# One recurrent-attention kernel: three groups of TensorE products run as two 64-column tiles of the array instead of one full-width product

## The chip, the core and the metric

The kernel runs on one NeuronCore of one Trainium2 chip. A core has five engines that run side by side and wait for each other through semaphores: TensorE (PE, matrix products; the profile lists its weight loads apart as PEld), VectorE (DVE), ScalarE (ACT), GpSimd (POOL) and SyncE (SP, which here only issues DMAs). The metric is device time in microseconds (us) for one execution; lower is better. All data are 32-bit floats, and TensorE does every such product in two passes: in the trace each product of the program stands as two weight loads (LDWEIGHTS) and two MATMULs, a transpose as one of each.

## What is computed

A gated linear recurrence, and behind it a layer norm with a two-layer MLP and a residual. The sizes are batch 4, 8 heads, 768 tokens, 48 values per head, model width 384 and hidden width 1536.

```python
for t in range(S):
    state = alpha[:, :, t, :, None] * state + np.einsum('bhd,bhe->bhde', k[:, :, t], v[:, :, t])
    y[:, :, t] = np.einsum('bhd,bhde->bhe', q[:, :, t], state)
x = y.transpose(0, 2, 1, 3).reshape(B, S, H * D)
xn = (x - mean) / np.sqrt(var + 1e-06) * g_ln
out = x + np.maximum(xn @ w_ch1, 0.0) @ w_ch2
```

## The kernel before

The 768 tokens are cut into 6 chunks `c` of 128 (`NCB`), and a chunk's attention is done for each of the 4 batches `b` in six steps. Two heads always share a 128-wide slot: head 0 of a pair lies in positions 0 to 47, head 1 in 64 to 111, and the rest are zeros. There are 4 pairs `p` (`NP`).

- `decays` (lines 167 to 187): logarithm of alpha (ACT), a product with a triangle of ones for running sums (`lps`, line 173), two exponentials, q and k times those (`qks`), and two small DMAs that turn the last row of the decay into the columns `gate`. It also issues the loads of the next chunk.
- `turn` (line 194): eight transposes into `tps`, copied to `qkT` by ACT and DVE.
- `scores` (line 209): q times k per head into `aps`. Its two heads use rows 0 to 47 and 64 to 111 of the array, so they are two row tiles side by side. DVE keeps the lower triangle (`at`, line 212).
- `attend`: into `yps`, per pair, the state's part (line 221: stationary `qkT`, 128 columns; moving `sts`, 96 columns; chunks 1 to 5 only) and per head the scores' part (line 225: stationary `at`, 128 columns; moving v, 48 columns). Then x (ACT, line 228), the norm's statistics (DVE and ACT, lines 231 to 235) and the normed `xn` (DVE, line 237).
- `turn_x` (line 247): three transposes into `xps`, and DVE writes them to `xT` (line 248), which holds all four batches.
- `update` (line 257, chunks 0 to 4): per pair `sps`, k times v (stationary 128 columns, moving 96). It also makes products across the two heads of a pair, which aren't wanted. POOL makes `gm` (line 262), the gate times a mask `own` that is zero for those; DVE adds `sps` to the state `sts` (line 267; in chunk 0 it copies, line 265), and POOL multiplies the state by `gm` (line 268).

The MLP of a chunk has 12 steps `hidden` (line 278: 3 products of 512 columns, into `hps`, then a ReLU by ACT or DVE in turn) and 12 steps `project` (line 291: 4 products of 384 columns each, three steps to a batch, into `ops`, then DVE adds x, line 295). `hidden` needs `xT` of all four batches.

The order is written out by `run(main, side)`: behind every step of `main` it issues as many steps of `side` as keep the two lists level. `attention_steps` lists the steps in waves (`stages[w - b]` for batch `b` in wave `w`), so with 4 batches and 6 stages there are 24 steps. While the MLP of chunk `c` is `main` (24 steps), the attention of chunk `c+1` is `side` (24 steps). At the start the attention of chunk 0 is `main` and the rounding of the MLP's weights, which arrive as 64-bit floats, is `side` (seven DVE operations for a piece, lines 127 to 136). In the MLP of chunk 0, 6 of the 24 side steps go with the 12 `hidden` steps and 18 with the 12 `project` steps.

```python
            due = (i + 1) * len(side) // len(main)
            for go in side[done:due]:
                go()
```

The framework that builds the program from this text may move an instruction ahead of others on its engine where those have to wait. PSUM buffers with the tag `s` (`yps`, `sps`, `xps`) are two.

Of the kernel before, what the change touches and what calls it, by code (L numbers as in the profile page):

```python
# [9 lines left out]
FP32 = mybir.dt.float32  # L10
# [11 lines left out]
def kernel(  # L22
# [23 lines left out]

    nc = tc.nc

    B, S, H, D = q.shape
    DM = H * D
    DF = w_ch1.shape[1]
    P = 128
    NCB = S // P
    NP = H // 2
    NF = DM // P
    NJ = DF // P
    assert S % P == 0 and H % 2 == 0 and D <= 64 and DM % P == 0 and DF % P == 0
# [11 lines left out]

    r = np.arange(P)
    upto = (r[None, :] >= r[:, None]).astype(np.float32)
    half = np.stack([r < 64, r >= 64], 1).astype(np.float32)
    const_np = np.concatenate([upto, np.eye(P, dtype=np.float32), half], 1)

    raws = {}

# [4 lines left out]
            nc.sync.dma_start(t, src[b, c * P:(c + 1) * P])  # L83
            raws[n, c, b] = t

    consts = cpool.tile([P, 2 * P + 2], FP32, name="consts")
    nc.scalar.dma_start(consts, nc.inline_tensor(const_np, name="consts").ap())
    tri, ident, own = consts[:, :P], consts[:, P:2 * P], consts[:, 2 * P:]
# [73 lines left out]

    gate_of, qkT_of, at_of, x_of, xn_of, xT_of, hT_of = ({} for _ in range(7))
# [3 lines left out]
    def decays(c, b):  # L167
# [12 lines left out]
        if c + 1 < NCB:  # L180
            row = dram.tile([1, NP, P], FP32, name="row", tag="row")
            gate = work.tile([P, NP], FP32, name="gate", tag="gate", bufs=B)
# [4 lines left out]
            load(c + 1, b)  # L187

    def turn(c, b):
        qkT = work.tile([P, 2, NP, P], FP32, name="qkT", tag="qkT", bufs=3)  # L190
        for i in range(2):
            tps = ps.tile([P, NP, P], FP32, name="tps", tag="a", bufs=3)
            for p in range(NP):
                nc.tensor.transpose(tps[:, p], qks[b][:, i, p].rearrange("p a b -> p (a b)"),  # L194
                                    ident)
            if i == 0:
                nc.scalar.copy(out=qkT[:, i], in_=tps)
            else:
                nc.vector.tensor_copy(out=qkT[:, i], in_=tps)  # L199
        qkT_of[c, b] = qkT  # L200
# [13 lines left out]
        at_of[c, b] = at  # L214

    def attend(c, b):
        qkT, at, vt = qkT_of.pop((c, b)), at_of.pop((c, b)), raws["v", c, b]
        yps = ps.tile([P, NP, 2, D], FP32, name="yps", tag="s")
        for p in range(NP):
            if c > 0:  # L220
                nc.tensor.matmul(yps[:, p].rearrange("p a b -> p (a b)"), qkT[:, 0, p],  # L221
                                 sts[b][:, p].rearrange("p a b -> p (a b)"),
                                 start=True, stop=False)
            for i in range(2):
                nc.tensor.matmul(yps[:, p, i], at[:, i, p], vt[:, 2 * p + i],  # L225
                                 start=(c == 0), stop=(c == 0 or i == 1))
        x = work.tile([P, DM], FP32, name="x", tag="x", bufs=2 * B)
        nc.scalar.copy(out=x, in_=yps.rearrange("p a b d -> p (a b d)"))  # L228
        stats = work.tile([P, 6], FP32, name="stats", tag="stats")
        mv = work.tile([P, 2], FP32, name="mv", tag="mv")  # L230
        nc.vector.bn_stats(stats, x)  # L231
# [3 lines left out]
        nc.scalar.activation(out=rstd, in_=rstd, func=AFT.Exp, scale=-0.5)  # L235
        xn = work.tile([P, DM], FP32, name="xn", tag="xn", bufs=2)
        nc.vector.tensor_scalar(out=xn, in0=x, scalar1=mv[:, 0:1], scalar2=rstd,
                                op0=AOP.subtract, op1=AOP.mult)
        x_of[c, b], xn_of[c, b] = x, xn

    def turn_x(c, b):
        if b == 0:
            xT_of[c] = work.tile([P, NF, B, P], FP32, name="xT", tag="xT")
        xn = xn_of.pop((c, b))
        xps = ps.tile([P, NF, P], FP32, name="xps", tag="s")
        for f in range(NF):
            nc.tensor.transpose(xps[:, f], xn[:, f * P:(f + 1) * P], ident)  # L247
        nc.vector.tensor_mul(xT_of[c][:, :, b], xps,
                             g_col.unsqueeze(2).broadcast_to([P, NF, P]))

    def update(c, b):
        vt = raws.pop(("v", c, b))
        if c == NCB - 1:
            return
        sps = ps.tile([P, NP, 2, D], FP32, name="sps", tag="s")
        for p in range(NP):
            nc.tensor.matmul(sps[:, p].rearrange("p a b -> p (a b)"),  # L257
                             qks[b][:, 1, p].rearrange("p a b -> p (a b)"),
                             vt[:, 2 * p:2 * p + 2].rearrange("p a b -> p (a b)"),
                             start=True, stop=True)  # L260
        gm = work.tile([P, NP, 2], FP32, name="gm", tag="gm")
        nc.gpsimd.tensor_mul(gm, gate_of.pop((c, b)).unsqueeze(2).broadcast_to([P, NP, 2]),
                             own.unsqueeze(1).broadcast_to([P, NP, 2]))
        if c == 0:
            nc.vector.tensor_copy(out=sts[b], in_=sps)  # L265
        else:
            nc.vector.tensor_add(sts[b], sps, sts[b])  # L267
        nc.gpsimd.tensor_mul(sts[b], sts[b],  # L268
                             gm.unsqueeze(3).broadcast_to([P, NP, 2, D]))

# [87 lines left out]
```

## Time and profile before

| what | value |
|---|---|
| time, median of 3 runs | 578.32 us (572.75 to 579.47) |
| the profiled execution | 577.86 us |
| its span, first to last instruction | 576.1 us |
| mean granted TensorE clock | 0.964 |
| PE busy | 547.2 us, 95%, 2408 MATMULs |
| PEld busy | 342.1 us, 59%, 2408 loads |
| DVE busy | 222.7 us, 39% |
| ACT busy | 90.2 us, 16% |
| POOL busy | 55.2 us, 10% |

The busy shares are means over stages that differ. "Chain" below is the chain of work that ended last: the profile follows it back from the last instruction, at each step to what released it or to the instruction before it on its engine. A MATMUL's own duration in the trace (about 0.28 us for a small one) holds its way through the array; several are in flight at once, so the time that one costs in a row of them is read from the start of one to the start of the next, or from the chain.

### The profile page before, as it was taken

The page shows a single profiled execution, that of the slowest core. Times are in us where ns is not written, and L with a number is a line of the kernel's source. Part 1 is how long each engine was busy: PE and PEld are TensorE (multiplying, and loading weights), DVE is VectorE, ACT ScalarE, POOL GpSimd, SP SyncE. Part 2 cuts the span into 40 slices and gives each one's busy share as a digit, 9 for nine tenths or more (in the row PEclk, how much of TensorE's full clock was granted, in tenths as well). Part 3 has the DMA queues.
Part 4 walks back from the last instruction along what each step waited for, and adds up shares of the span by engine and source line. Part 5 has one row for each costly group of instructions (what it writes and reads, how often), then busy time and mean ns, then how long its engine had stood idle before and what let it go on. Part 6 is the DMA issues. An engine that isn't in the chain of part 4 may idle for free.

```text
span 576.1 us, 5992 instructions
## 1 busy us (share of the span) xinstructions
PE 547.2 (95%) x2408; PEld 342.1 (59%) x2408; DVE 222.7 (39%) x365; ACT 90.2 (16%) x205; POOL 55.2 (10%) x70
## 2 busy tenths in 40 slices
PE   4876897999999999999999999999999999999997
PEld 2675443667746567755567656566755566644453
DVE  3997997533343232233332223423223332211100
ACT  3311121111122200032210032210013210001000
POOL 2111131000110000020000120000111000000000
PEclk9865799999999999999999999999999999999999
DMA  8874433110231100032100122000000000000000
GB/s 284 285 213 133 151 109 96 43 56 27 65 87 42 41 28 29 27 91 62 41 21 22 41 70 69 28 1 28 14 15 0 1 0 22 21 14 0 0 29 27
DMA packets 32484, 33.64 MB, mean 58 GB/s; under 512 B 13108, under 2 KB 28596, under 8 KB 32456
## 3 DMA queue, kind: packets, MB, share of 16 engines
q1 hardware_dynamic: 31912, 33.12, 18.8%
q8 instruction: 19, 0.31, 0.2%
q10 hardware_dynamic: 544, 0.13, 0.1%
q14 instruction: 9, 0.07, 0.0%
HBM read 28.49 MB, written 4.76 MB: 58 GB/s over the span
## 4 chain that ended last, share of the span: by engine, by line
PE 84%; DVE 9%; DMA 5%; SPq 1%; issue 0%; ACT 0%; ACTq 0%
PE ops L291 33%; PE hps L278 28%; PE yps L225 7%; PE aps L209 4%; PE yps L221 3%; PE tps L194 3%; PE sps L257 3%; PE lps L173 2%; DMA row<-eq 2%; DVE ws L135 1%; DVE w L129 1%; DMA rv<-in_v_dram 1%; PE xps L247 1%; DMA ws<-in_moe_w_ch_dram 1%; DVE w L136 1%; DVE ws L134 1%
## 5 line engine op out<-in xcount | busy, mean ns | idle before, releaser
L278 PE MATMUL hps<-xT,w 128*128 128x512 f32 x432 | 198.3, 602 | 3.6 <-DVE hT L283 3.6
L291 PE MATMUL ops<-w,hT 128*128 128x384 f32 x576 | 198.7, 491 | 2.0 <-DVE ob L295 2.0
L291 PEld LDWEIGHTS ops<-w,hT 128*128 128x128 f32 x576 | 104.7, 190 | 66.0 <-DVE ob L295 4.1
L278 PEld LDWEIGHTS hps<-xT,w 128*128 128x128 f32 x432 | 80.4, 193 | 89.3 <-issue 78.3
L225 PE MATMUL yps<-rv,at 128*128 128x48 f32 x384 | 58.5, 283 | 2.4 <-DVE st L265 1.9
L225 PEld LDWEIGHTS yps<-rv,at 128*128 128x128 f32 x384 | 54.8, 209 | 3.8 <-DVE st L265 2.3
L283 DVE TENSOR_SCALAR hT<-hps 128x512 f32<-128x512 f32 x36 | 24.8, 690 | 57.7 <-PE hps L278 57.7
L178 POOL TENSOR_TENSOR qk<-rk,ek 128x384 f32<-128x384 f32 x24 | 30.2, 1259 | 165.3 <-ACT ek L176 160.4
L281 ACT ACTIVATE hT<-hps 128x512 f32<-128x512 f32 x36 | 21.5, 597 | 148.7 <-PE hps L278 148.7
L231 DVE BATCH_NORM_STATS2 stats<-x 128x6 f32<-128x384 f32 x24 | 13.4, 560 | 73.1 <-ACT x L228 73.1
L179 DVE TENSOR_TENSOR qk<-rq,eq 128x384 f32<-128x384 f32 x24 | 24.1, 1002 | 41.3 <-ACT eq L177 41.3
L228 ACT COPY x<-yps 128x384 f32<-128x384 f32 x24 | 11.5, 479 | 172.8 <-PE yps L225 172.8
L212 DVE COPY_PREDICATED at<-consts,aps 128x512 f32<-128x512 int32 x48 | 32.5, 717 | 13.5 <-PE aps L209 13.5
L268 POOL TENSOR_TENSOR st<-st,gm 128x384 f32<-128x384 f32 x20 | 18.1, 904 | 202.6 <-DVE st L267 181.3
L295 DVE TENSOR_TENSOR ob<-ops,x 128x384 f32<-128x384 f32 x24 | 13.4, 558 | 61.8 <-PE ops L291 61.8
L209 PEld LDWEIGHTS aps<-qkT 48*128 48x128 f32 x384 | 25.9, 202 | 16.9 <-issue 10.3
L209 PE MATMUL aps<-qkT 48*128 48x128 f32 x384 | 31.0, 302 | 3.0 <-DVE qkT L199 3.0
L194 PEld LDWEIGHTS tps<-consts,qk 128*128 128x128 f32 x192 | 23.5, 148 | 16.4 <-issue 8.2
L221 PE MATMUL yps<-st,qkT 128*128 128x96 f32 x160 | 32.7, 286 | 0.0
L194 PE MATMUL tps<-consts,qk 128*128 128x128 f32 x192 | 27.6, 286 | 4.9 <-DVE qk L179 4.2
L221 PEld LDWEIGHTS yps<-st,qkT 128*128 128x128 f32 x160 | 25.6, 192 | 6.2 <-issue 3.8
L199 DVE COPY qkT<-tps 128x512 f32<-128x512 f32 x24 | 16.6, 690 | 31.5 <-PE tps L194 31.5
(34 smaller groups left out, 281.8 us busy)
## 6 DMA issues: line engine op xcount, KB each, us to landing
ws<-in_moe_w_ch_dram SPq DMA_DIRECT2D x12, 768.0 KB
ra<-in_alpha_dram SPq DMA_DIRECT2D x24, 192.0 KB
rk<-in_k_dram SPq DMA_DIRECT2D x24, 192.0 KB
rq<-in_q_dram SPq DMA_DIRECT2D x24, 192.0 KB
rv<-in_v_dram SPq DMA_DIRECT2D x24, 192.0 KB
out_dram<-ob SPq DMA_DIRECT2D x24, 192.0 KB
row<-eq SPq DMA_DIRECT2D x20, 2.0 KB
gate<-row SPq DMA_DIRECT2D x20, 2.0 KB
```

Of the source, the lines that this page charges most:

```text
L178: nc.gpsimd.tensor_mul(qk[:, 1, :, :D], raws.pop(("k", c, b)), ek)
L179: nc.vector.tensor_mul(qk[:, 0, :, :D], raws.pop(("q", c, b)), eq)
L194: nc.tensor.transpose(tps[:, p], qks[b][:, i, p].rearrange("p a b -> p (a b)"), ident)
L209: nc.tensor.matmul(aps[i][:, p], qkT[rows, 1, p], qkT[rows, 0, p], start=True, stop=True)
L212: nc.vector.copy_predicated(out=at[:, i], data=aps[i], mask=mask.unsqueeze(1).broadcast_to([P, NP, P]))
L221: nc.tensor.matmul(yps[:, p].rearrange("p a b -> p (a b)"), qkT[:, 0, p], sts[b][:, p].rearrange("p a b -> p (a b)"), start=True, stop=False)
L225: nc.tensor.matmul(yps[:, p, i], at[:, i, p], vt[:, 2 * p + i], start=(c == 0), stop=(c == 0 or i == 1))
L268: nc.gpsimd.tensor_mul(sts[b], sts[b], gm.unsqueeze(3).broadcast_to([P, NP, 2, D]))
L278: nc.tensor.matmul(hps, w1[:, f, j * P:(j + 1) * P], xT_of[c][:, f], start=(f == 0), stop=(f == NF - 1))
L281: nc.scalar.activation(out=hT_of[c][:, j], in_=hps, func=AFT.Relu)
L283: nc.vector.tensor_scalar_max(hT_of[c][:, j], in0=hps, scalar1=0.0)
L291: nc.tensor.matmul(ops_of[b], hT_of[c][:, j, b], w2[:, j], start=(j == 0), stop=(j == NJ - 1))
```

## The change

The 128 columns of a stationary operand are cut in two halves of 64, each of which goes to its own half of the array's columns and writes its own 64 partitions of PSUM.

- `attend`: each product of lines 221 and 225 becomes two, one for tokens 0 to 63 and one for tokens 64 to 127 (`sides`), with the same moving operand. Of the 128 rows of the state's part 112 are used (`R`).
- The update moves from its own step into `attend`, right behind the products of y. Instead of one product per pair there is one per head (moving 48 columns instead of 96): head 0 on columns 0 to 63, head 1 on 64 to 111. The products across heads are no longer made, so the mask `own` and `gm` go. DVE adds in two pieces of 64 and 48 partitions, in chunk 0 as well, for which POOL clears `sts` at the start. POOL multiplies the state by the gate directly.
- `turn`: `qkT` and `tps` have 112 partitions instead of 128.
- `attention_steps`: five stages, 20 steps instead of 24, so `run` spreads them differently.

```diff
+    R = 64 + D
...
-    consts = cpool.tile([P, 2 * P + 2], FP32, name="consts")
+    consts = cpool.tile([P, 2 * P], FP32, name="consts")
...
+        nc.gpsimd.memset(sts[b], 0.0)
...
-        qkT = work.tile([P, 2, NP, P], FP32, name="qkT", tag="qkT", bufs=3)
+        qkT = work.tile([R, 2, NP, P], FP32, name="qkT", tag="qkT", bufs=3)
         for i in range(2):
-            tps = ps.tile([P, NP, P], FP32, name="tps", tag="a", bufs=3)
+            tps = ps.tile([R, NP, P], FP32, name="tps", tag="a", bufs=3)
             for p in range(NP):
-                nc.tensor.transpose(tps[:, p], qks[b][:, i, p].rearrange("p a b -> p (a b)"),
-                                    ident)
+                nc.tensor.transpose(
+                    tps[:, p], qks[b][:, i, p].rearrange("p a b -> p (a b)")[:, :R], ident)
...
+        sides = [slice(64 * s, 64 * s + 64) for s in range(2)]
         for p in range(NP):
             if c > 0:
-                nc.tensor.matmul(yps[:, p].rearrange("p a b -> p (a b)"), qkT[:, 0, p],
-                                 sts[b][:, p].rearrange("p a b -> p (a b)"),
-                                 start=True, stop=False)
+                for s in sides:
+                    nc.tensor.matmul(yps[s, p].rearrange("p a b -> p (a b)"), qkT[:, 0, p, s],
+                                     sts[b][:R, p].rearrange("p a b -> p (a b)"),
+                                     start=True, stop=False)
             for i in range(2):
-                nc.tensor.matmul(yps[:, p, i], at[:, i, p], vt[:, 2 * p + i],
-                                 start=(c == 0), stop=(c == 0 or i == 1))
+                for s in sides:
+                    nc.tensor.matmul(yps[s, p, i], at[:, i, p, s], vt[:, 2 * p + i],
+                                     start=(c == 0), stop=(c == 0 or i == 1))
+        if c + 1 < NCB:
+            sps = ps.tile([R, NP, D], FP32, name="sps", tag="s")
+            heads = list(enumerate((slice(0, 64), slice(64, R))))
+            for p in range(NP):
+                for i, s in heads:
+                    nc.tensor.matmul(sps[s, p], qks[b][:, 1, p, i, :s.stop - s.start],
+                                     vt[:, 2 * p + i], start=True, stop=True)
+            for i, s in heads:
+                nc.vector.tensor_add(sts[b][s, :, i], sps[s], sts[b][s, :, i])
+            st = sts[b].rearrange("p a b d -> p a (b d)")
+            nc.gpsimd.tensor_mul(
+                st, st, gate_of.pop((c, b)).unsqueeze(2).broadcast_to([P, NP, 2 * D]))
         x = work.tile([P, DM], FP32, name="x", tag="x", bufs=2 * B)
         nc.scalar.copy(out=x, in_=yps.rearrange("p a b d -> p (a b d)"))
...
-    def update(c, b):
...
-        sps = ps.tile([P, NP, 2, D], FP32, name="sps", tag="s")
-        for p in range(NP):
-            nc.tensor.matmul(sps[:, p].rearrange("p a b -> p (a b)"),
-                             qks[b][:, 1, p].rearrange("p a b -> p (a b)"),
-                             vt[:, 2 * p:2 * p + 2].rearrange("p a b -> p (a b)"),
-                             start=True, stop=True)
-        gm = work.tile([P, NP, 2], FP32, name="gm", tag="gm")
-        nc.gpsimd.tensor_mul(gm, gate_of.pop((c, b)).unsqueeze(2).broadcast_to([P, NP, 2]),
-                             own.unsqueeze(1).broadcast_to([P, NP, 2]))
-        if c == 0:
-            nc.vector.tensor_copy(out=sts[b], in_=sps)
-        else:
-            nc.vector.tensor_add(sts[b], sps, sts[b])
-        nc.gpsimd.tensor_mul(sts[b], sts[b],
-                             gm.unsqueeze(3).broadcast_to([P, NP, 2, D]))
...
-        stages = [decays, turn, scores, attend, turn_x, update]
+        stages = [decays, turn, scores, attend, turn_x]
```

More of the change, by code (lines that the diff above doesn't have):

```diff
@@ L73 @@
     upto = (r[None, :] >= r[:, None]).astype(np.float32)
-    half = np.stack([r < 64, r >= 64], 1).astype(np.float32)
-    const_np = np.concatenate([upto, np.eye(P, dtype=np.float32), half], 1)
+    const_np = np.concatenate([upto, np.eye(P, dtype=np.float32)], 1)
     raws = {}
@@ L84, in load @@
             raws[n, c, b] = t
-    consts = cpool.tile([P, 2 * P + 2], FP32, name="consts")
+    consts = cpool.tile([P, 2 * P], FP32, name="consts")
     nc.scalar.dma_start(consts, nc.inline_tensor(const_np, name="consts").ap())
-    tri, ident, own = consts[:, :P], consts[:, P:2 * P], consts[:, 2 * P:]
+    tri, ident = consts[:, :P], consts[:, P:]
     mask = tri.bitcast(INT32)
@@ L216, in attend @@
     def attend(c, b):
-        qkT, at, vt = qkT_of.pop((c, b)), at_of.pop((c, b)), raws["v", c, b]
+        qkT, at, vt = qkT_of.pop((c, b)), at_of.pop((c, b)), raws.pop(("v", c, b))
         yps = ps.tile([P, NP, 2, D], FP32, name="yps", tag="s")
+        sides = [slice(64 * s, 64 * s + 64) for s in range(2)]
         for p in range(NP):
             if c > 0:
-                nc.tensor.matmul(yps[:, p].rearrange("p a b -> p (a b)"), qkT[:, 0, p],
-                                 sts[b][:, p].rearrange("p a b -> p (a b)"),
-                                 start=True, stop=False)
+                for s in sides:
+                    nc.tensor.matmul(yps[s, p].rearrange("p a b -> p (a b)"), qkT[:, 0, p, s],
+                                     sts[b][:R, p].rearrange("p a b -> p (a b)"),
+                                     start=True, stop=False)
             for i in range(2):
-                nc.tensor.matmul(yps[:, p, i], at[:, i, p], vt[:, 2 * p + i],
-                                 start=(c == 0), stop=(c == 0 or i == 1))
+                for s in sides:
[13 more added lines that the diff above has]
+                st, st, gate_of.pop((c, b)).unsqueeze(2).broadcast_to([P, NP, 2 * D]))
         x = work.tile([P, DM], FP32, name="x", tag="x", bufs=2 * B)
```

3 lines of the change are left out of this document (removed).

## The prediction

> **What bounds the kernel now.** I read the page first (span, busy times, chain), then the windows by stage, then the chain around one `attend`. Page:
>
> ```profile
> span 576.1 us, 5992 instructions
> PE 547.2 (95%) x2408; PEld 342.1 (59%) x2408; DVE 222.7 (39%) x365; ACT 90.2 (16%) x205; POOL 55.2 (10%) x70
> PE 84%; DVE 9%; DMA 5%; SPq 1%; issue 0%; ACT 0%; ACTq 0%
> ```
>
> TensorE is busy for 95% and holds 84% of the chain. The windows split this by stage (after each window: its length, then busy time and instructions of PE, PEld, DVE, ACT, POOL, then the granted clock):
>
> ```profile
> 0.00:62.00 62.00, 42.10 (x214) 34.89 (x215) 48.21 (x82) 14.79 (x34) 12.79 (x19) 0.72 0.70 217
> 62.00:99.00 37.00, 33.44 (x102) 15.84 (x101) 33.13 (x53) 6.04 (x11) 8.23 (x3) 0.96 0.40 131
> 334.20:422.80 88.60, 88.60 (x413) 55.61 (x413) 28.15 (x46) 14.75 (x34) 8.15 (x12) 1.00 0.12 34
> ```
>
> A whole chunk in the middle takes 88.60 us and PE is busy for all of it; DVE has 28.15 us to do there. What PE is spared here comes off the time, one for one. Up to 99 us it is different: DVE, which rounds weights, is busy 81.3 of 99 us, PE has gaps, and the clock is at 0.72 at first. So the middle must be priced product by product. The chain gives the time that each group takes in the stream (start, length, group):
>
> ```profile
> 344.08 2.57 PE hps L278 x6
> 346.65 1.09 PE aps L209 x16
> 347.74 2.77 PE hps L278 x6
> ...
> 354.61 2.57 PE hps L278 x6
> 357.19 0.20 PE yps L221 x2
> 357.38 0.41 PE yps L225 x4
> 357.79 0.26 PE yps L221 x2
> ...
> 359.39 0.41 PE yps L225 x4
> 359.80 2.64 PE hps L278 x6
> ```
>
> ```profile
> 299.78 0.86 PE sps L257 x8
> ```
>
> Three prices come out. **A streamed column:** six hps MATMULs of 512 columns take 2.57 us, 0.428 each, 0.84 ns a column; so 48 columns stream in 0.040 us, 96 in 0.080, 128 in 0.107. **A weight load of 128 columns:** the 24 yps MATMULs of one `attend` take 2.61 us (357.19 to 359.80), 0.109 each, though 16 of them stream only 48 columns; the eight sps (96 columns) take 0.108 each. Both are above their streams and equal: these products wait for the next load, not for the stream. **A change of tiling:** aps runs as two row tiles. Its 16 MATMULs are 8 pairs of 0.107 us, 0.86 in all, if the two tiles run wholly side by side; in the chain they take 1.09, and the hps behind them 2.77 instead of 2.57. So 1.29 - 0.86 = 0.43 us go to getting into the tiled form and out again. That 8 pairs fit at all shows that loads and streams of two row tiles run together.
>
> **The change, part by part.**
>
> *Products, chunks 1 to 4 (16 times).* Before: 2.61, plus 0.07 on the hps behind (2.64 against 2.57), plus 0.86 for sps: 3.54 us. After: 8 pairs for the state's part (4 `p` x 2 passes), 16 pairs for the scores' part, 8 for the update; MATMULs rise from 32 to 64. No row shows a load of 64 columns. It can take nothing less than its stream hides (0.040 for 48 columns) and no more than the whole 0.109. I take half, 0.055, since the loads of aps, with 48 rows instead of 128, fit 0.107 too: rows aren't what is paid for, so columns are. Nor does a row show two column tiles at once. A pair costs 0.055 if they run side by side and 0.109 if the loads take turns; I take the former by aps, the only tiled row there is. The state's pairs are then held by their stream, 0.080. Sum: 8 x 0.080 + 16 x 0.055 + 8 x 0.055 = 1.96, plus one change of tiling, 0.43: 2.39 us. Saved: 1.15 us, 16 times, **18.4 us**.
>
> The Trainium skill (TensorE: Matmul & The Clock Gate, section LDWEIGHTS (loading the stationary operand)) makes a load's time its columns over 1.2, so 53 ns for 64: no row here shows it, and by it the sum would be about 1 us lower (448 narrow pairs by 0.002).
>
> *Chunk 5 (4 times).* There is no update: 2.68 before, 0.64 + 0.88 + 0.43 = 1.95 after, 0.73 saved, **2.9 us**.
>
> *The start.* In the first 62 us DVE waits for what stands behind the slow products:
>
> ```profile
> L237 DVE TENSOR_SCALAR xn<-x,mv,rstd 128x384 f32<-128x384 f32 x4 | 3.1, 771 | 2.4 <-ACT rstd L235 2.4
> L231 DVE BATCH_NORM_STATS2 stats<-x 128x6 f32<-128x384 f32 x4 | 2.2, 556 | 1.5 <-ACT x L228 1.5
> ```
>
> At most these 3.9 us can go; the DVE additions below cost up to 0.7 back, since DVE is the bound there. I take **1 us** saved.
>
> *DVE and POOL.* The groups of the whole run (busy us, mean ns of one):
>
> ```profile
> L283 DVE TENSOR_SCALAR hT<-hps 128x512 f32<-128x512 f32 x36 | 24.8, 690 | 57.7 <-PE hps L278 57.7
> L268 POOL TENSOR_TENSOR st<-st,gm 128x384 f32<-128x384 f32 x20 | 18.1, 904 | 202.6 <-DVE st L267 181.3 <-DVE st L265 21.3
> L267 DVE TENSOR_TENSOR st<-sps,st 128x384 f32<-128x384 f32 x16 | 8.9, 558 | 15.1 <-PE sps L257 15.1
> L262 POOL TENSOR_TENSOR gm<-gate,consts 128x8 f32<-128x8 f32 x20 | 4.9, 247 | 37.1 <-DMA gate<-row 36.3
> L265 DVE COPY st<-sps 128x384 f32<-128x384 f32 x4 | 2.2, 541 | 0.0
> ```
>
> The addition of 384 columns (0.558 us) becomes two of 192, each between 0.28 and 0.56. From 512 to 384 columns 0.13 us go, so I take 0.36 each, 0.16 more per step; with 28 of 88.6 us busy, DVE has room. If that room were gone, it would be 16 x 0.16 + 4 x 0.18 = 3.3 us. POOL loses `gm` (4.9 us) and gets four memsets ahead of its first product: no time, as POOL is busy for 10% of the span only. The state is ready a whole chunk before the next product needs it, so the earlier wait for `gate` costs nothing; behind that multiplication on POOL stands `decays`' k product of a later batch, which PE asks for only a step further on. DMAs are the same.
>
> *The order.* Here is a loss. `turn_x` of batch 3 is now the last of 20 side steps and falls behind the last `project`; `hidden` of the next chunk needs its `xT`. Before, `update` of batch 3 lay between:
>
> ```profile
> 155.43 0.49 PE L247 MATMUL xps<-consts,xn 128*128 128x128 f32 x3
> ...
> 155.75 1.03 PE L257 MATMUL sps<-rv,qk 128*128 128x96 f32 x8
> 156.10 0.55 DVE L248 TENSOR_TENSOR xT<-xps,g_col 128x384 f32<-128x384 f32 x1
> ...
> 156.62 0.84 PE L173 MATMUL lps<-la,consts 128*128 128x384 f32 x2
> ...
> 157.29 3.17 PE L278 MATMUL hps<-xT,w 128*128 128x512 f32 x7
> ```
>
> The xps end at 155.75, when the next group starts, and DVE has `xT` ready at 156.65: 0.9 us that sps covered. After, PE meets them uncovered at five chunk boundaries. The lps of the next `decays` (156.62 to 157.29, 0.67) stood ahead of hps here already and can fill most: I take 0.2 each. At the boundary from chunk 0 to 1 (14 side steps over 12) `attend` and `turn_x` of batch 3 even follow each other with no MLP step between. From y to `xn` it takes:
>
> ```profile
> 359.83 0.48 ACT L228 COPY x<-yps 128x384 f32<-128x384 f32 x1 [2.01 <-PE yps L225]
> ...
> 361.72 0.48 DVE L237 TENSOR_SCALAR xn<-x,mv,rstd 128x384 f32<-128x384 f32 x1 [0.60 <-ACT rstd L235]
> ```
>
> That is 2.4 us, and some 0.7 more with the two additions ahead of the statistics on DVE; the update's products and the way out of the tiles cover about 0.65, so 2.5 are open. At the other boundaries a `project` third (2.6 us) covers this. Together 2.5 + 5 x 0.2 = **3.5 us lost**; 0 if more is moved up, 6.7 if lps isn't.
>
> **Sum** on the profiled execution (577.86 us: its span and 1.76 around it; the median of the runs is 578.32): 577.86 - 18.4 - 2.9 - 1.0 + 3.5 = **559 us**.
>
> **The rivals.** The two halves differ from aps in one thing: row tiles take different partitions, column tiles read the same 128. So each of these is open.
>
> 1. *The halves take turns*, loads and streams: 0.109 for a narrow pair, 0.161 for the state's. Chunks 1 to 4: 24 x 0.109 + 8 x 0.161 + 0.43 = 4.33 against 3.54, 16 times; chunk 5: 16 x 0.109 + 1.29 + 0.43 = 3.46 against 2.68, 4 times; with 3.5 lost and about 1 at the start this is +20: **598 us, slower**. Against it speaks aps, for it only the shared partitions. The point from which this decides: at 0.092 for a pair (448 narrow and 160 state pairs) the gain is zero.
> 2. *The loads alone bring nothing* (in turns, or 64 columns as dear as 128): 0.109 for every pair, +0.38 sixteen times, +0.37 four times, 3.5 and 0.5: **589 us**.
> 3. *The streams alone take turns*: 0.080 and 0.161: 3.64 against 3.54, 3.00 against 2.68, 3.5: **584 us**.
> 4. *Issue binds.* Four instructions per 0.055 us are one per 14 ns; the densest stretch of the trace, aps, has 32 in 0.86, 27 ns. Were that the limit, 128 would take 3.44 + 0.43 and 96 2.58 + 0.43: +6.6 and 3.5, **588 us**. What is queued while the hps run ahead would soften this; no row says how much.
> 5. *A load can't run beside a stream in the same rows.* A narrow pair is then 2 x (0.055 + 0.040) = 0.19, the state's 0.27: 7.15 against 3.54 and 5.63 against 2.68: **651 us**. The rows speak against it: by that rule the 24 yps before would take 16 x 0.149 + 8 x 0.189 = 3.9 us, and they take 2.61. The rule is that of the Trainium skill (TensorE: Matmul & The Clock Gate, section The mechanism): weight loads pass running products only where the row groups differ, which two column tiles don't offer. By that rule the change loses 13%; the trace disagrees with it where it can be read.
>
> **How the numbers follow.** Forecast 0.62, rival 1 0.08, rival 2 0.08, rival 3 0.08, rival 4 0.10, rival 5 0.02, others 0.02. The forecast's own range: down to 549 (no loss in the order, all 3.9 us at the start, narrow pairs somewhat under 0.055), up to 567 (lps not moved up, nothing at the start, pairs at 0.062). For 8 in 10 it must reach over rivals 3 and 4: 549 to 589, leaving out 1, 5 and half of 2. About 2%, 11.6 us, is what a measurement tells from no change: faster needs 566.7 or less, which is nine tenths of the forecast (0.56) and a softened rival 4 (0.04), 0.60. Slower by over 2%: rivals 1, 5 and half of 2, and some of the others, 0.15. Within: 0.25.
>
> **What would show it.** In the changed profile: 64 MATMULs of one `attend` in the chain at about 2 us, with 0.4 beside them; narrow loads starting in twos, 0.055 apart; a middle chunk at about 84.2 instead of 88.6 us (1.15 x 4 less, 0.2 more); DVE `xT` as PE's releaser at five boundaries with 0.2 to 0.9 us each, and about 3 at the first. Wrong it would be if the pairs are 0.09 apart or more, if other instructions are put into the group so that the tiling changes more than once, or if the order loses more than 7 us.

## The result and the profile after

The changed kernel takes **558.48 us** (median of 4 runs, 557.12 to 560.75). The kernel before took 575.67 us on the same chip (median of 4, 572.75 to 579.47). The ratio is **0.9702**, with a 95% interval of 0.9623 to 0.9781. The forecast was 559 us. The profiled execution of after took 557.12 us, the shortest of the four. One execution of experiment 1 (3171 us) and one of experiment 9 (2960 us) took five times as long as the others of their kernels and are left out of the times below.

The page of after, span and busy times, then its chain by engine:

```profile
span 555.3 us, 7418 instructions
PE 519.0 (93%) x3112; PEld 303.0 (55%) x3112; DVE 225.0 (41%) x385; ACT 90.1 (16%) x205; POOL 50.4 (9%) x54
PE 88%; DVE 7%; DMA 3%; issue 1%; POOL 0%; SPq 0%; POOLq 0%; DVEq 0%
```

There are 704 more MATMULs, and PE is busy for 28 us less. TensorE is still the bound; its share of the chain has risen from 84% to 88%.

The windows of after (length, then busy time and instructions of PE, PEld, DVE, ACT, POOL, then the granted clock): the start, the first `hidden`s, the whole chunk in the middle that answers to the 88.60 us of the prediction, and the chunk in which the attention of chunk 5 is made.

```profile
0.00:61.50 61.50, 33.26 (x310) 24.71 (x310) 49.99 (x88) 14.88 (x34) 17.85 (x19) 0.73 0.72 224
61.50:98.70 37.20, 37.20 (x108) 17.86 (x109) 36.41 (x57) 6.04 (x11) 1.00 (x1) 0.95 0.37 123
319.20:404.03 84.83, 84.82 (x540) 49.58 (x540) 28.66 (x50) 14.73 (x34) 7.30 (x8) 1.00 0.12 34
404.03:487.03 83.00, 82.21 (x475) 47.59 (x475) 25.73 (x42) 13.91 (x32) 4.00 (x4) 1.00 0.03 10
```

The same stretches of before, from the first hps of a chunk to the first of the next, and its `hidden`s of chunk 0:

```profile
62.07:103.79 41.72, 38.14 (x110) 18.00 (x110) 37.75 (x59) 6.04 (x11) 8.23 (x3) 0.93 0.36 116
333.99:422.68 88.69, 88.69 (x415) 55.70 (x413) 28.15 (x46) 14.75 (x34) 8.15 (x12) 1.00 0.12 34
422.68:507.85 85.17, 85.17 (x383) 52.17 (x381) 25.82 (x42) 13.92 (x32) 4.84 (x5) 1.00 0.03 10
```

A middle chunk went from 88.69 to 84.83 us, so 3.86 less; the forecast had 4.4 less. The next one went from 85.17 to 83.00, 2.17 less. And 4.5 us went where nothing was expected: `hidden` of chunk 0 took 41.72 us and now takes 37.20, with PE busy for all of it. Over the whole span, 576.1 to 555.3, 20.8 us went where the sum had 18.8. That the total is so near the forecast needs looking into: several terms of the sum and the time that it started from were off, and they partly cancel.

The chain of after through one `attend` (start, length, group):

```profile
174.74 2.57 PE hps L276 x6
177.32 0.32 PE yps L226 x4
177.63 0.22 PE yps L231 x8
177.85 0.18 PE yps L226 x4
...
178.83 0.22 PE yps L231 x8
179.05 0.46 PE sps L238 x14
179.51 2.77 PE hps L276 x6
```

From 177.32 to 179.51 are 2.19 us, and the hps behind take 2.77 instead of 2.57: 2.39 us for the whole group, which is the forecast to the digit. Eight narrow MATMULs (4 pairs) take 0.22, so 0.055 a pair. The state's 2 pairs take 0.18, so 0.09 and not 0.080. The update's 8 pairs take about 0.46 (the chain puts 14 of the 16 under that name). That makes 0.72 + 0.88 + 0.46 = 2.06; the other 0.13 lie at the first state pairs, where the tiled form is entered.

The rows of one load show what made it possible (after, the line of the scores' part: shortest, middle and longest duration in ns):

```profile
L231 PEld LDWEIGHTS yps<-rv,at x768: 132/138/232, 16.0 to 482.9; 128*64 128x64 f32 x192
```

One load is 138 ns long in the trace, and a new pair of them begins every 55 ns or so: the rows of several loads overlap. The duration of one row is not its price in the stream, as with MATMULs.

### The profile page after: what moved, and what is told of

Its sections match the earlier page's. It is cut to its first block, busy times and chain, and to the rows that moved or that the text cites. A ratio compares the mean times of both kernels' runs of the same rounds, so it can differ in the third digit from the quotient of the medians.

```text
span 555.3 us, 7418 instructions
## 1 busy us (share of the span) xinstructions
PE 519.0 (93%) x3112; PEld 303.0 (55%) x3112; DVE 225.0 (41%) x385; ACT 90.1 (16%) x205; POOL 50.4 (9%) x54
## 4 chain that ended last, share of the span: by engine, by line
PE 88%; DVE 7%; DMA 3%; issue 1%; POOL 0%; SPq 0%; POOLq 0%; DVEq 0%
PE ops L289 35%; PE hps L276 34%; PE aps L212 4%; PE yps L231 4%; PE yps L226 3%; PE tps L197 3%; PE lps L176 2%; PE sps L238 1%; PE xps L265 1%; DMA ws<-in_moe_w_ch_dram 1%; DVE ws L137 1%; DVE w L131 1%; DVE w L129 1%; DVE w L138 1%; DMA ra<-in_alpha_dram 1%
## 5 line engine op out<-in xcount | busy, mean ns | idle before, releaser
L276 PE MATMUL hps<-xT,w 128*128 128x512 f32 x432 | 195.8, 601 | 1.8 <-DVE xT L266 1.8
L215 DVE COPY_PREDICATED at<-consts,aps 128x512 f32<-128x512 int32 x48 | 32.5, 719 | 18.9 <-PE aps L212 18.8
L231 PE MATMUL yps<-rv,at 128*64 128x48 f32 x768 | 39.8, 230 | 0.0
L231 PEld LDWEIGHTS yps<-rv,at 128*64 128x64 f32 x768 | 35.5, 149 | 3.9 <-issue 3.9
L241 DVE TENSOR_TENSOR st<-sps,st 64x192 f32<-64x192 f32 (+1 forms) x40 | 14.2, 355 | 57.0 <-PE sps L238 56.7
L243 POOL TENSOR_TENSOR st<-st,gate 128x384 f32<-128x384 f32 x20 | 18.6, 928 | 182.4 <-DVE st L241 151.4
L197 PE MATMUL tps<-consts,qk 128*112 128x128 f32 x192 | 27.8, 286 | 7.2 <-DVE qk L182 5.4
L197 PEld LDWEIGHTS tps<-consts,qk 128*112 128x112 f32 x192 | 22.9, 139 | 19.4 <-issue 9.7
L176 PE MATMUL lps<-la,consts 128*128 128x384 f32 x48 | 22.1, 544 | 8.2 <-ACT la L174 4.3
L226 PE MATMUL yps<-st,qkT 112*64 112x96 f32 x320 | 29.7, 259 | 0.0
L202 DVE COPY qkT<-tps 112x512 f32<-112x512 f32 x24 | 16.5, 689 | 31.3 <-PE tps L197 31.3
```

The source lines that it names most:

```text
L176: nc.tensor.matmul(lps[:, :DM], tri, la, start=True, stop=True)
L215: nc.vector.copy_predicated(out=at[:, i], data=aps[i], mask=mask.unsqueeze(1).broadcast_to([P, NP, P]))
L226: nc.tensor.matmul(yps[s, p].rearrange("p a b -> p (a b)"), qkT[:, 0, p, s], sts[b][:R, p].rearrange("p a b -> p (a b)"), start=True, stop ...
L231: nc.tensor.matmul(yps[s, p, i], at[:, i, p, s], vt[:, 2 * p + i], start=(c == 0), stop=(c == 0 or i == 1))
L276: nc.tensor.matmul(hps, w1[:, f, j * P:(j + 1) * P], xT_of[c][:, f], start=(f == 0), stop=(f == NF - 1))
```

## The experiments

The chunk times below are from the first hps of chunk 3 to the first of chunk 4, where the clock is 1.00 and nothing of the start is left; before has 88.69 there and after 84.83. Ratios are to the kernel before, run on the same chip.

**1. The order alone.** Before, with `update` called inside `attend` and taken from the stages: the new order, with full-width products.

```diff
+        update(c, b)
         x = work.tile([P, DM], FP32, name="x", tag="x", bufs=2 * B)
...
-        stages = [decays, turn, scores, attend, turn_x, update]
+        stages = [decays, turn, scores, attend, turn_x]
```

> The update stands in attend, right behind y, and there are 20 side steps instead of 24; all products are full width as before. Theory (the gain is the two halves running at once): no product gets cheaper, and the chunk boundaries lose what they lose in the changed kernel (about 3 us at the first, 0.5 at the others): 3 to 6 us slower than the kernel before, or level with it if the 3.6 us stall at 95 to 99 us of the first profile is missing. Rival (the gain is the new order): 10 us or more faster.

582.72 us (581.50 to 584.10, three runs), ratio 1.0109 (1.0011 to 1.0206); a chunk takes 89.12, 0.43 more than before. Its chain at a chunk boundary:

```profile
334.22 2.62 PE ops L292 x8
...
336.87 0.36 DVE ob L296
...
337.35 0.56 DVE xT L249
...
337.95 7.13 PE hps L279 x16
```

TensorE has ended its `project` at 336.84 and starts `hidden` at 337.95. Between them the chain runs over DVE: the addition `ob` of the last `project` step stands in DVE's queue ahead of `xT`. This is the loss in the order that the prediction named. By itself the new order makes the kernel slower, by 0.1 to 2.1%. Not all of that is the boundaries: against the span of experiment 5's kernel, which has no stall at the start (571.1 us), 9.8 us are added, of them 4.0 ahead of the first hps, 5.1 from there to the end of chunk 0 with its boundary, and about 0.4 in each of chunks 2 to 4. The expectation had said level with before if the stall at the start is missing. Here it is nearly missing (TensorE is idle for 0.6 us at that place instead of 3.6), and the kernel is slower all the same.

**2. y alone in halves.** After, with `update` full-width again and a step of its own (24 steps, the old order).

```diff
-        if c + 1 < NCB:
-            sps = ps.tile([R, NP, D], FP32, name="sps", tag="s")
...
-        stages = [decays, turn, scores, attend, turn_x]
+        stages = [decays, turn, scores, attend, turn_x, update]
```

> Only y and the state's part run in halves; the update is a step of its own at full width, the order is that of the kernel before. Theory: 2.68 us become 1.95 for each of 20 groups, no loss in the order: 14.6 us faster than the kernel before, about 560. Rival (the order brings the gain): within 3 us of the kernel before.

557.91 us, ratio 0.9678 (0.9603 to 0.9752): as much as the whole change, though two of its four runs lie at an upper level, and the profiled one of these carries the stall that experiment 5 is about. A chunk takes 85.70, so the 4 groups save 2.99, 0.75 each.

**3. The update alone in halves,** inside `attend`, with y full-width. The diff is the first part of the change's, undone.

```diff
-                for s in sides:
-                    nc.tensor.matmul(yps[s, p].rearrange("p a b -> p (a b)"), qkT[:, 0, p, s],
-                                     sts[b][:R, p].rearrange("p a b -> p (a b)"),
-                                     start=True, stop=False)
+                nc.tensor.matmul(yps[:, p].rearrange("p a b -> p (a b)"), qkT[:, 0, p],
+                                 sts[b][:R, p].rearrange("p a b -> p (a b)"),
+                                 start=True, stop=False)
...
```

> Only the update runs in halves, in attend, with 20 side steps; y and the state's part are full width. Theory: the update falls from 0.89 to 0.44 us, and one change of tiling (0.43) is now paid for it alone: nothing gained by the products, and the boundaries' loss is there: 2 to 6 us slower than the kernel before (level if the stall at the start is missing). Rival (the update, with its unwanted products gone, is the gain): 5 us or more faster.

580.34 us over 10 runs, ratio 1.0072 (1.0038 to 1.0107); a chunk takes 88.54. Its chain behind one `attend`:

```profile
331.05 0.59 PE sps L235 x14
331.65 2.78 PE ops L286 x8
```

Alone, the update in halves costs 0.59 and another 0.20 on the product behind it: 0.79 where the full-width one had 0.86 and up to 0.03 behind it. It pays for its own change of tiling, and nearly nothing is left. The whole kernel stays within 2% of before.

**4. The halves one behind the other.** After, with all products of tokens 0 to 63 first and then those of tokens 64 to 127; the same for the update's two heads. The same instructions in another program order.

```diff
-        for p in range(NP):
-            if c > 0:
-                for s in sides:
+        for s in sides:
+            for p in range(NP):
+                if c > 0:
...
-            for p in range(NP):
-                for i, s in heads:
+            for i, s in heads:
+                for p in range(NP):
```

> The changed kernel with the same products in another order: all of the first half's of an attend, then all of the second half's; the update likewise. Theory (two halves in flight at once are the gain, and the engine takes products in program order): the group takes 2 x (8 x 0.080 + 16 x 0.055) + 2 x 8 x 0.055 + 0.43 = 4.35 us instead of 2.39 in chunks 1 to 4 and 3.47 instead of 1.95 in chunk 5: 37 us slower than the changed kernel, about 595. Rival (64-column loads alone are the gain, or the engine pulls the second half's products ahead): about as the changed kernel, 558.

588.74 us, ratio 1.0218 (1.0155 to 1.0282). The windows' row of its chunk, then its chain at the seam between the two halves:

```profile
339.87:430.34 90.47, 90.47 (x541) 55.17 (x541) 28.66 (x50) 14.74 (x34) 7.32 (x8) 1.00 0.11 31
```

```profile
368.75 0.22 PE yps L230 x4
368.97 0.18 PE yps L226 x2
369.15 0.04 PE yps L230
369.20 0.06 PE yps L226
```

Within a half, four narrow MATMULs take 0.22, 0.055 for one instead of for a pair: each load of 64 columns costs half of a load of 128 (0.109), and no second tile runs beside it. Only at a seam, where the last few products of one half meet the first of the other, do rows of both interleave. So the two tiles ran side by side only where the program alternates between them within a few instructions. A chunk is 5.64 us longer than after, 1.41 a group. The expectation had 1.96 a group and 595 us: it had left out the overlap at the seams, of which a group has three (between the halves of y, from y to the update, and between the update's heads).

**5. Before, with one product moved.** The chain of before held 9% on DVE and 5% on DMA, and the first `hidden`s had 3.6 us of idle TensorE. The product of k and its decay, which POOL makes, had one row of 6.83 us. Here the k product of chunk 1, batch 0 goes to DVE.

```diff
-        nc.gpsimd.tensor_mul(qk[:, 1, :, :D], raws.pop(("k", c, b)), ek)
+        (nc.vector if (c, b) == (1, 0) else nc.gpsimd).tensor_mul(qk[:, 1, :, :D], raws.pop(("k", c, b)), ek)
```

> The kernel before, with one instruction moved: the k product (line 178) of chunk 1, batch 0 runs on DVE instead of POOL. Theory (the start's gain is that this POOL product, 6.83 us instead of 1.00 among back-to-back DVE work, held up the next weight load; it happens in some executions of the kernel before and is not what the change removes): every run at 572 to 574 us, none at 578. Rival (the change itself shortens the start): runs at 573 and 578 as before, or all near 578.

572.40 us in 10 runs (571.42 to 573.84), ratio 0.9944 (0.9908 to 0.9981). The 13 runs of before beside it lie at two levels, 572.6 to 573.8 (6 runs) and 576.9 to 579.4 (7); of these 10 none is at the upper one. The timeline of before at the place, then the windows' row of the same stretch (PE, PEld, DVE, ACT, POOL busy):

```profile
81.06 6.83 POOL L178 TENSOR_TENSOR qk<-rk,ek 128x384 f32<-128x384 f32 x1 [17.04 <-ACT ek L176]
...
86.95 0.68 DVE L283 TENSOR_SCALAR hT<-hps 128x512 f32<-128x512 f32 x1
...
87.92 0.35 SPq L83 DMA_DIRECT2D rk<-in_k_dram  x1
...
88.85 0.38 SPq L115 DMA_DIRECT2D ws<-in_moe_w_ch_dram  x1
...
95.13 0.56 DVE L127 TENSOR_SCALAR w<-ws 128x768 int32<-128x768 int32 x1 [3.87 <-DMA ws<-in_moe_w_ch_dram]
```

```profile
81.06:87.89 6.83, 6.83 (x30) 3.36 (x29) 6.83 (x12) 1.32 (x3) 6.83 (x1) 1.00 0.18 74
```

And TensorE's own row in before, behind it:

```profile
99.03 4.28 PE L278 MATMUL hps<-xT,w 128*128 128x512 f32 x6 [3.58 <-DVE hT L283]
```

The windows' row behind that gap, with the granted clock third from the end:

```profile
99.00:102.00 3.00, 2.98 (x4) 1.43 (x5) 2.94 (x5) 0.00 (x0) 0.00 (x0) 0.51 0.00 0
```

A product that mostly takes 1.00 us lasts 6.83 while DVE is busy without a gap (6.83 of 6.83 us, 12 operations with those at the edges). SP's load of the next k goes out at 87.92, as the product ends, and the load of a piece of weights stands behind it in SP's queue: issued at 88.85, and DVE waits 3.87 us for it. TensorE is idle for 3.58 us, and its next six hps take 4.28 us instead of 2.57, as the granted clock is 0.51 there. In the edited kernel:

```profile
81.36 1.28 POOL L178 TENSOR_TENSOR qk<-rk,ek 128x384 f32<-128x384 f32 x1 [17.63 <-ACT ek L176]
...
83.96 0.38 SPq L115 DMA_DIRECT2D ws<-in_moe_w_ch_dram  x1
```

The row at 81 us is there too: it is the product of batch 1, still on POOL, and not the one that was moved. The edit shifted the engines' work by some tenths of a us (this row starts 0.3 later), and the same product took 1.28 us; the weights' load went out 4.9 us earlier. So in these two profiles the stall goes with that one long product; that the moved product was its cause is not shown. Nor is a long product enough for the whole stall. Experiment 1 has one of 5.82 us at the same place, but there the weights' load stands right behind that of k; DVE waits 1.9 us for it, and TensorE 0.6. After has the product at the same place with 1.00 us:

```profile
81.30 1.00 POOL L181 TENSOR_TENSOR qk<-rk,ek 128x384 f32<-128x384 f32 x1 [25.71 <-ACT ek L179]
```

The traces suggest what decides whether POOL gets through, though no run tests it. The three long products (in before and in experiments 1 and 2) start within 0.08 us of the start of a DVE operation, and end 0.93 to 0.95 us after the start of the first later one that reads PSUM (`hT`, at 86.95 above). The two short ones start some 0.35 us ahead of the next DVE operation, and it is that one which then takes 0.5 to 0.8 us longer than its like.

Experiment 2 has both levels again: two runs at 555.3 and 555.5, two at 560.3 and 560.7, and its profiled run, one of the latter, has such a product of 6.77 us. The 4 runs of after and 4 more of the same kernel (experiment 8) all lie within 557.1 and 560.8.

**6. The attention ends one step earlier.** After, with `run` spreading the side steps over one main step less in the MLP, so that `turn_x` of batch 3 falls ahead of the last `project`.

```diff
-            due = (i + 1) * len(side) // len(main)
+            due = min(len(side), -(-(i + 1) * len(side) // (len(main) - early)))
...
```

> The changed kernel, with the attention steps spread so that the last of them comes one MLP step before the end of the MLP. Theory (turn_x of batch 3 standing last costs about 0.5 us at each boundary and about 3 at the first): 3 to 5 us faster than the changed kernel, 554 to 555. Rival (the boundaries cost nothing, since lps fills them): 558 as the changed kernel.

553.04 us (552.31 to 553.25), ratio 0.9598 (0.9518 to 0.9679); a chunk takes 84.27, 0.56 less than after. By the medians it gains 5.4 us on after, by order alone; the two profiled spans differ by 3.8, as that of after is its shortest run. The chain of after in that chunk shows two things that are gone here:

```profile
319.20 7.99 PE hps L276 x18
...
380.60 0.32 PE yps L226 x4
380.92 0.21 PE yps L231 x6
381.13 5.36 PE ops L289 x16
386.49 0.19 PE yps L231
```

First, 18 hps at the head of the chunk take 7.99 instead of 18 x 0.4292 = 7.73: 0.26, behind the wait for `xT`. Second, and not looked for: the group of one `attend` is **cut in two**. Ten of its MATMULs are followed by 16 of `project`, and the rest come behind those. TensorE gets into the tiled form twice: the 16 ops take 5.36 instead of 5.16, and the first product behind them 0.19 instead of about 0.05, some 0.35 together. With the 0.26 that is 0.61 for the 0.56 measured. The chain of after shows such a cut once in each chunk's MLP from 1 to 4 (5.36 us for 16 ops at 211.47, 296.30, 381.13, 465.04); that of finish_early shows none in its four attends of the chunk, and one in chunk 0's MLP (at 137.96). Why the program puts the instructions in that order was not traced.

**7. The attend of one batch and the scores of the next as one step,** on top of 6: the update's products and those of `scores` are both tiled, and nothing comes between them.

```diff
-        return [lambda f=stages[w - b], b=b: f(c, b)
...
+            if s == 2 and out_steps and out_steps[-1][-1] == (3, b - 1):
+                out_steps[-1].append((s, b))
...
```

> As the last one, and attend of a batch and scores of the next are one step, so that the column tiles are left straight into the row tiles of aps. Theory (each way in or out of a tiled form costs about 0.2 us): about 0.2 us less for each of 15 to 18 such neighbours, 3 us faster than the one with the early finish, about 552. Rival (a change from one tiling to another costs as much as two): no difference.

554.01 us, ratio 0.9623 (0.9555 to 0.969). A chunk takes 83.67, 0.60 less than in 6; but the first hps of chunk 0 starts at 65.4 us, where 6 has it at 62.9, and this eats the gain: 3 us less than in 6 were expected, and it is 1.0 more. Its chain:

```profile
298.34 0.46 PE sps L238 x14
298.80 1.09 PE aps L212 x16
299.89 2.78 PE ops L289 x8
```

The aps stand right behind the sps, row tiles behind column tiles, and only the ops after them pay 0.20: three such neighbours in a chunk, 0.2 each, are the 0.60.

**8. The update in halves as a step of its own,** with y in halves, and the unedited changed kernel once more.

```diff
-        if c + 1 < NCB:
-            sps = ps.tile([R, NP, D], FP32, name="sps", tag="s")
...
-        stages = [decays, turn, scores, attend, turn_x]
+        stages = [decays, turn, scores, attend, turn_x, update]
```

> The changed kernel, with the update in halves as a step of its own again (24 side steps). Theory: it pays a second change of tiling, 0.44 + 0.43 = 0.87 against 0.89 at full width: a middle chunk takes 85.7 us as in the kernel with y alone in halves (85.70), against 84.83 in the changed kernel. Rival (a change of tiling is paid once per chunk or costs nothing on its own): 84 us or less.

> The changed kernel itself, for comparison on the same chip: 557 to 561 us, whichever of its two levels (573 or 578) the kernel before shows.

The update apart: 552.26 us in a single run; a chunk takes 85.28, so 0.42 less than with the full-width update (experiment 2), 0.1 a group, and 1.0 more than with the update behind y in an otherwise undisturbed order (experiment 6), 0.25 a group. Its start is the shortest of the kernels so far, the first hps at 57.9 us. The changed kernel again: 558.80 us, ratio 0.9669 (0.9598 to 0.974).

**9. Four tiles of 32 columns.** After, with four `sides`; the update's heads are cut at 32 too.

```diff
-        sides = [slice(64 * s, 64 * s + 64) for s in range(2)]
+        sides = [slice(32 * s, 32 * s + 32) for s in range(4)]
...
```

> The changed kernel with four tiles of 32 columns instead of two of 64. Theory (a narrow group costs the longer of its load, by columns, and its stream, however many tiles run; issue has room): a set of four takes the stream's 0.043 us instead of 0.0585 for a pair, the state's stay at 0.08: about 0.3 us less for each of 20 groups, 5 to 7 us faster than the changed kernel, 552. Rival (issue binds: one instruction per 14.6 ns is the densest seen): eight instructions take 0.117, about 30 us slower, 590.

550.88 us (550.55 to 552.38, four runs), ratio 0.9531 (0.9462 to 0.9601). Its profile is that of the execution of 2960 us, so only its time is used here, and the profile of the fourfold tiles is read in the next kernel.

**10. What the runs point to.** The halves; the update behind y from chunk 1 on, and a step of its own in chunk 0; the early end of 6; the joined steps of 7 from chunk 1 on. Then the same with four tiles of 32.

```diff
+        if c > 0:
+            update(c, b)
...
+        stages = [decays, turn, scores, attend, turn_x] + ([update] if c == 0 else [])
```

> What the runs point to: y and the state's part in halves, the update in halves behind y from chunk 1 on but as a step of its own in chunk 0 (update_apart has the shortest start, 57.9 us to the first hidden), the early finish, and scores of the next batch straight behind attend (not in chunk 0). Theory: start 58, then 85.4, three chunks at 83.7, 81.6 and 68.2, and 1.8 around it: 546 to 548 us. Rival (the start isn't set by where the update stands): 551 to 553.

> The last version with four tiles of 32 columns instead of two of 64. Theory (as for the quarters alone: 0.37 us less for a group with update, 0.3 without): the two gains add up, 546.7 - 7 = 539 to 541 us, and the loads of a narrow set stand 0.043 to 0.045 us apart instead of 0.0585. Rival (the gain of the quarters was in the order or the start): 546 to 547.

Halves: **546.68 us**, ratio 0.9456 (0.9396 to 0.9515). Quarters: **539.52 us**, ratio 0.9369 (0.9298 to 0.944). Chain and loads of the latter (in the loads' row: busy us and mean ns, then idle time):

```profile
270.24 0.30 PE yps L226 x8
270.54 0.17 PE yps L231 x16
...
271.73 0.34 PE sps L269 x32
```

```profile
L231 PEld LDWEIGHTS yps<-rv,at 128*32 128x32 f32 x1536 | 28.3, 114 | 5.9 <-issue 5.0 <-DVE at L215 0.9
```

Sixteen narrow MATMULs take 0.17: four sets of four, 0.0425 a set, where 48 columns stream in 0.040. Now these too are held by the stream, and the state's by theirs (0.085). A chunk takes 82.20, 1.47 less than with halves: 0.37 a group.

## Why the forecast held, step by step

*The price of a pair: right.* This carried the forecast, and it had been taken between far ends. Narrow pairs take 0.055, the group 2.39. That the group agrees to the digit is luck: the state's pairs were 0.01 too cheap (0.08 a group) and the update's together 0.02, while the way into the tiled form and out again takes 0.13 + 0.20 = 0.33 and not 0.43. Of what the whole of after saves in a group without the order's losses, 1.105 ((88.69 - 84.27) / 4) for the forecast 1.15, 0.75 comes from y and the state, 0.10 from the update's halves, and 0.25 from putting the update behind y, where it shares their change of tiling. The last 0.25 stood in the sum only inside "one change of tiling".

*The rivals 1, 2, 3 and 5: shown wrong.* Halves that take turns were made on purpose (experiment 4): 0.055 for one narrow product, 588.74 us. It shows at once that the load of 64 columns is half of 128's (against rival 2). With the program alternating, a pair costs what one costs alone, so neither loads nor streams take turns (1 and 3).

Rival 5 was a rule of the Trainium skill (TensorE: Matmul & The Clock Gate, section The mechanism): weight loads pass running products only where the row groups differ. The two column tiles share their rows, and a pair costs 0.055 where that rule gives 0.19: the trace disagrees. The same section also lets a load for the background weight buffer pass; whether that is what happens here, no run shows.

*Rival 4, issue: shown wrong.* Four instructions per 0.055 us were the question. Four tiles of 32 put eight (four loads, four MATMULs) into 0.0425, one per 5.3 ns, without a loss.

*Chunk 5: right.* 2.9 forecast; 85.17 to 82.19 us, 2.98, in finish_early, whose order is not disturbed. The 2.17 of after is this less the order's loss.

*The order: mis-sized, 3.5 forecast, about 4.8 measured,* by the difference between after and finish_early from the first `project` on (2.9 at the first boundary with the chunk behind it, then 0.55, 0.56 and 0.81). The first boundary was sized well for this execution. The chain of after there:

```profile
147.42 0.82 POOL st L243
148.24 1.36 POOL qk L181
...
149.65 0.43 PE tps L197 x2
...
151.28 1.77 PE hps L276 x4
```

From the end of sps, 146.36, to 151.28 are 4.92 us, of which the transposes (tps 0.87, xps 0.33) and two lps (1.30) fill 2.50; 2.42 are empty where 2.5 were expected. But the chain runs not over `xn` alone: it runs over the multiplication of the state on POOL and the k product queued behind it, for which the transposes wait. The prediction had named just these two and let them go, as something "which PE asks for only a step further on"; at this place there is no step between. `xn` ended at 149.81 in any case, so this cost little more.

The second profile of the same kernel (after_again) shows what the sum didn't have. The same gap is there, but behind it the granted clock is 0.57 from 150 to 152 us, where after has 1.00 throughout: two lps take 1.28 us instead of 0.65, and the next two hps 0.85 each instead of 0.43. The first boundary with its chunk then costs 4.5 instead of 2.9, and the order 6.4 us in all. So what this gap costs differs from one execution to the next.

The later boundaries were taken at 0.2 and cost 0.56 to 0.81. In the chunk read above, the wait for `xT` is 0.26 of that, near the forecast; the other part is the cut in the group, which stood in the prediction under what would make it wrong and had no price in the sum.

*The start and DVE: 1.0 saved forecast.* In the two profiled executions the first hps came 0.6 us earlier. Among the kernels profiled (without experiment 9) it lies between 57.6 and 65.8 us, from 3.9 us before that of after to 4.2 behind it; the sum had no term for that. What sets it was not settled, but the profiles fall apart by one thing: where the update of chunk 0 is a step of its own and y runs in halves, the first hps starts at 57.6 to 59.2; where the update stands in `attend`, at 61.5 to 65.8; before and the kernel of experiment 5, with both at full width, have 62.1 and 61.8. DVE's two half additions cost nothing that can be seen: DVE is busy for 28.66 us of a chunk instead of 28.15.

*The base of the sum: not seen.* The sum started from 577.86 us, an execution of the upper of two levels. Some 4.5 us of it were the stall of experiment 5, which is none of the change's doing; a row of 8.23 us for 3 POOL instructions stood in the prediction's own windows and was not followed. Against before without that stall (before_k_on_dve), the spans go from 571.1 to 555.3: 15.8 us, of 18.8 forecast. By terms: products 16 x 1.105 = 17.7, chunk 5 2.98, start 0.3 (61.8 to 61.5), order -4.8, together 16.2. For the second profile of after (span 557.0) it is 14.1 us measured, and by terms, with -0.2 at the start and -6.4 for the order, 14.1 as well. So the forecast landed at 559 because too large a gain was taken from too high a base: the mechanism was right, and the closeness of the number is luck. The claim itself holds on either base: 558.48 is 2.4% below the 572.40 of before_k_on_dve and more below the upper level.

## What to carry to other kernels

Where small products wait for their loads, cut the stationary operand's columns into tiles of the array, alternate between the tiles instruction by instruction, and put tiled groups next to each other, since here each way out costs 0.2 us. Go on cutting until the stream is the bound: here halves gave 0.055 and quarters 0.0425 per set where 48 columns stream in 0.040. Before summing from one profile, see whether the runs of the kernel fall into groups, find in which one the profile lies, and follow every row that lasts several times longer than its like.

## What the runs showed of the hardware that was not expected

**A POOL operation can last through many DVE operations.** It took 6.83 us instead of 1.00, while DVE ran 12 operations back to back; in after and in the edited kernel the same product took 1.00 and 1.28 us. The Trainium skill (SBUF — State Buffer, section SBUF: two separate sides) says that DVE and GpSimd share one pair of ports, which a GpSimd operation, or a DVE operation with two inputs in SBUF or in a two-port mode, holds for its whole instruction while the other engine is blocked. The traces fit this: after a short product it is the DVE operation behind it that lasts longer, and a long one ends with the first `hT`, which reads PSUM. But the wait went through eight or nine operations and not one, and that DVE causes it is read from the order of the rows; no run took DVE's work away.

**Tiles do not keep the program's order among themselves.** The timeline of after at the end of the attend that was cut:

```profile
387.66 0.22 PE L238 MATMUL sps<-rv,qk 128*64 128x48 f32 x1
387.71 0.22 PE L231 MATMUL yps<-rv,at 128*64 128x48 f32 x1
```

The update's first product starts 0.05 us ahead of the last one of y, which stands before it in the kernel's text. In experiment 4 products of the second half start ahead of the last ones of the first in the same way. In the first boundary's group of after (its update around 146 us) the MATMULs of the head with 48 columns start 0.045 us apart and those of the head with 64 columns 0.058; the former are through at 146.02, ahead of the last two of the latter (146.05 and 146.11), which both stand before it in the text. It looks as if each tile had a stream of its own that may run ahead by a few products. No run tested how far, and the traces hold starts only: that the framework left these instructions in the order of the text is not shown.
